# Attention and Fourier mixing on one core: where the row pass of the softmax throws its exponentials

## The chip, the cores and the metric

The kernel runs on 1 core of one Trainium2 chip. The metric is the device time of one execution in microseconds (us). Before the change it is 2742.67 us, the median of 3 runs (2741.53 to 2744.46).

## The reference, cut to what matters

```
# x: 2048 x 1024, 32 heads of 32, one key/value head for all of them
q = heads(x @ wq);  k = x @ wk;  v = x @ wv
scores = einsum("bhqd,bkd->bhqk", q, k) * 32 ** -0.5
p = softmax(scores, axis=-1)
a = heads_back(einsum("bhqk,bkd->bhqd", p, v)) @ wo
# a second, independent part on an input of its own (2048 x 1024)
y = seq_re @ (x2 @ hid_re) - seq_im @ (x2 @ hid_im)
out = concatenate([a, y], axis=-1)
```

Only the softmax is touched by the change. For each of the 32 x 2048 rows of scores it needs the row's largest score and the sum of the row's exponentials.

## The kernel before, in words

All work is written out in program order, engine by engine: the helper class `Ordered` (line 71) records every instruction, which is why the profile names one line, L79, for nearly all of them. Tiles are told apart by name instead.

The attention is cut into 32 *units* (4 blocks of 512 queries by 8 groups of 4 heads), and a unit into 32 *steps*, 1,024 in all. The main loop (line 941) runs one step n after the other, and does two things in a step, for two different units:

- **The row pass, ahead of time.** `score_step` (line 860) looks 44 steps ahead. `scores` (line 744) has TensorE make 128 queries x 1024 keys of scores in a PSUM tile `pss` (two matmuls; two such tiles exist), and VectorE takes each row's maximum into `nm`. One step later `row_sums` (line 755) has ScalarE take the exponential of that tile with the maximum as bias, with `accum_out` giving each row's sum. Only the sum is used. The exponentials themselves are thrown away: they are written back over the scores in `pss`. In the profile this instruction is a pair, ACTIVATE `pss<-pss,nm` and ACTIVATION_READ_ACCUMULATOR.
- **The exponentials by keys.** When a unit's row sums are known, `expo` (line 807) has TensorE make the scores again the other way round, 128 keys x 1024 queries, in the PSUM tile `pst` (two matmuls; only one such tile exists), and ScalarE takes their exponentials into an SBUF tile `p` (a pool `pp` of 13, line 719). In the profile: ACTIVATE `p<-pst`.

Within a step ScalarE's order is: the row pass of a step further ahead, then the exponentials by keys. TensorE's order is: the pss pair, the pst pair, then fill.

At steps 0, 12 and 22 of a unit, `pv` (line 821) has TensorE multiply the `p` tiles so far with the values: a *PV block* of 20 or 24 matmuls in the program, each of them two in the trace. This is what lets the `p` tiles go. Ahead of it, `aside` (line 405) may put up to six fill matmuls.

The *fill* is the rest of TensorE's work: projections, Fourier products and the output product, as matmuls `psb<-rh,mh` and the like. `level` (line 933) hands it out over the steps without a PV block, so that such a step holds four to six fill matmuls beside its pss and pst pairs. GpSimd prepares the fill's operands, SyncE's queue brings and takes data by DMA. The first 44 score steps run ahead of the main loop with seven fill matmuls each and without exponentials by keys; the last 44 steps of the main loop have no scores to make any more.

Order among instructions of different engines, and where a later instruction of the same engine overwrites what an earlier one wrote, is kept by semaphore waits that the tile layer puts in, one for each tile that is written or read.

Of the kernel before, what the change touches and what calls it, by code (L numbers as in the profile page):

```python
# [8 lines left out]
F32 = mybir.dt.float32  # L9
F32R = mybir.dt.float32r  # L10
AF = mybir.ActivationFunctionType
# [5 lines left out]
P = 128  # L17
# [4 lines left out]
W = 512  # L22
# [79 lines left out]
def tile_kernel(ctx: ExitStack, tc, xT, wq, wkv, wo, xbT, wT, cT, out):  # L102
    nc = tc.nc
    te = Ordered(tc, nc.tensor)
    act = Ordered(tc, nc.scalar)
# [5 lines left out]
    def pool(stack, name, bufs, **kw):  # L111
        kw.setdefault("reuse_waits", "tile")
        return stack.enter_context(tc.tile_pool(name=name, bufs=bufs, **kw))
# [36 lines left out]
    def move(q, to, of):  # L150
        q.dma_start(to.bitcast(F32), of.bitcast(F32))
# [125 lines left out]
    def add(gs):  # L277

        for g in gs:
            i0 = g.at = end[0]  # L280
            end[0] += g.n
            if groups and g.set[0] is not groups[-1].set[0]:
                prev["set"] = prev["this"]
                prev["this"] = i0
            for c, it in enumerate(g.right):
                if it.need is None:
                    it.need = i0 + 3 * c
                    p0 = min(prev["set"], i0 - it.back)
                    it.due = min(it.need, p0 + (i0 - p0) * (g.first + c + 1) // (len(g.set) * len(g.right))) - it.ahead
                    RL.items.append(it)  # L290
                it.last = i0 + 3 * c + 2
            for c, it in enumerate(g.left):
                if it.need is None:
                    it.need = it.due = i0 + 12 * c
                    ML.items.append(it)
                it.last = i0 + 12 * c + 11
            for it in g.ys:
                it.due = i0 + g.n
                ylist.append(it)
            groups.append(g)  # L300
# [31 lines left out]
    def store(to, of, key=None):  # L332
        def go():
            move(sp, to, of)
            if key:
                ready.add(key)
        soon(go)
# [240 lines left out]
    def wo_set(e):  # L578
        return [Item([(lambda g=g: wo[g * P:(g + 1) * P, e * W:(e + 1) * W], 1)]) for g in range(NG)]

    def o_left(b, t, q):
        g1 = min(q * 4 + 4, NQ * NG - 1 - b * NG)

        def src():
            assert all(("o", b, g) in ready for g in range(q * 4, g1)), (b, t, q)
            return [d[b][t][:, q * 4:g1] for d in (oh_d, ol_d)]
        return Item(None, pre=src)
# [82 lines left out]
    def o_group(b, t, e, ws):  # L670
        def post(ps):
            r0 = b * W + t * P
            to = out[r0:r0 + P, e * W:(e + 1) * W]
            if b < NQ - 1:
                oo = op.tile([P, W], F32, name="qh")
                dve.tensor_copy(oo, ps)
                store(to, oo)
                return

            n = len(halves)  # L680
            halves.append(n)
            oo = pp.tile([P, 2, W], F32, name="p")
            if n + 1 < 8:
                if n % 2:
                    dve.tensor_copy(oo[:, 0], ps)
                else:
                    act.activation(oo[:, 0], ps, AF.Copy)
                move(act, to, oo[:, 0])
                return
            for k, q in enumerate((act, sp)):  # L690
                cols = slice(k * W // 2, (k + 1) * W // 2)
                if k:
                    dve.tensor_copy(oo[:, k, :W // 2], ps[:, cols])
                else:
                    act.activation(oo[:, k, :W // 2], ps[:, cols], AF.Copy)
                move(q, to[:, cols], oo[:, k, :W // 2])
        return Group([o_left(b, t, q) for q in range(2)], ws, post)
# [21 lines left out]
    pp = pool(ctx, "pp", NP)  # L719
# [7 lines left out]
    qst, nm, lse, pt, ov, rb, pend = ({} for _ in range(7))  # L727
    ends = []

    def open_unit(u):  # L730
        b, g = units[u]
        assert ("q", b, g) in ready
        if u < 3:
            rows.append(qsp.tile([P, 4, W], F32R, name=f"qst{u}"))
            gp.memset(rows[u][96:P].bitcast(F32), 0.0)
        q = rows[u % 3]
        if u >= 3:
            move(sp, q[96:98].rearrange("p a b -> p (a b)"), kst[98:100])
        for r, src in enumerate((qh_d, ql_d, qh_d)):
            move(sp, q[r * DH:(r + 1) * DH], src[b][g].rearrange("(h d) c -> d h c", d=DH))  # L740
        qst[u] = q
        nm[u] = sm.tile([P, 10, NC], F32, name="nm")

    def scores(s):
        u, r = divmod(s, SU)
        i, j = divmod(r, 2)
        h, t = divmod(i, 4)
        ps = ps_s.tile([P, 2 * W], F32, name="pss")
        for a in range(2):
            k0 = (2 * j + a) * W  # L750
            te.matmul(ps[:, a * W:(a + 1) * W], qst[u][:, h, t * P:(t + 1) * P], kst[:, k0:k0 + W], start=True, stop=True)
        dve.tensor_reduce(nm[u][:, j, i:i + 1], ps, axis=AX.X, op=ALU.max, negate=True)
        pend[s] = ps

    def row_sums(s):
        if s not in pend:
            return
        ps = pend.pop(s)
        u, r = divmod(s, SU)
        i, j = divmod(r, 2)  # L760
        act.activation(ps, ps, AF.Exp, bias=nm[u][:, j, i:i + 1], accum_out=nm[u][:, 8 + j, i:i + 1])

    def over(rows):
        return rows.rearrange("p a c -> p c a")
# [21 lines left out]
    def lse_3(u):  # L786
        aside()
        pm = bank("psb")
        te.transpose(pm[:3 * NC, :P], nm[u][:, 3:6].rearrange("p a b -> p (a b)"), ident)
        mt = sm.tile([3 * NC, P], F32, name="mt")  # L790
        dve.tensor_copy(mt, pm[:3 * NC, :P])
        cur["at"] += 1
        lse[u] = mt
# [7 lines left out]
    def inverse(u):  # L801
        rb[u] = onp.tile([P, W], F32, name="rb")
        for h in range(4):
            r = r_d[u][4 * h:4 * h + 4].rearrange("t c -> (t c)")
            sp.dma_start(rb[u][h * DH:(h + 1) * DH], r.unsqueeze(0).to_broadcast([DH, W]))

    def expo(n):
        u, r = divmod(n, SU)
        c, hp_ = divmod(r, 2)
        pt[u, c, hp_] = pp.tile([P, 2, W], F32, name="p")  # L810
        ps = ps_t.tile([P, 2, W], F32, name="pst")
        for a in range(2):
            te.matmul(ps[:, a], kst[:, c * P:(c + 1) * P], qst[u][:, 2 * hp_ + a], start=True, stop=True)
        act.activation(pt[u, c, hp_], ps, AF.Exp)
# [45 lines left out]
    def score_step(s):  # L860

        if s < total:
            u, r = divmod(s, SU)
            if r == SU - 6 and u + 1 < len(units):
                open_unit(u + 1)
        if SU <= s < SU * (len(units) + 1) and s % SU == TURN:
            lse_3((s - SU) // SU)
        if s < total:
            scores(s)
        row_sums(s - 1)  # L870
        u, e = divmod(s - SU, SU)
        if 0 <= u < len(units):
            for f in LSE.get(e, ()):
                f(u)
# [58 lines left out]
    def level(n):  # L933
        r = n % SU
        if r in ENDS:
            return
        more = min(e for e in ENDS if e > r) - r
        left = goal(n + more) - pos["fill"]
        take(round(left / more))

    for n in range(total):
        u, r = divmod(n, SU)
        if n == total - 12:
            w1 = wo_set(1)
            add([o_group(NQ - 1, t, e, ws) for e, ws in ((0, w0), (1, w1)) for t in range(4)])
        score_step(n + SU + LEAD)
        if ends:
            ends.pop(0)()
        expo(n)
        if r == 16:  # L950
            inverse(u)
        if r in ENDS and n:
            pv((n - 1) // SU, (ENDS.index(r) - 1) % (len(CUT) - 1))
        level(n)
# [20 lines left out]
    def whole(i):  # L975
        if i % 5 < 2:
            return ps_s.tile([P, 2 * W], F32, name="pss")[:, :W]
        if i % 5 == 2:
            return ps_t.tile([P, 2, W], F32, name="pst")[:, 0]
        return ps_b[i % 5 - 3].tile([P, W], F32, name="psb")  # L980
# [9 lines left out]
    for t, g in enumerate(last[4:]):  # L990
        ps = whole(4 + t)
# [41 lines left out]
```

## Time and profile before

| | |
|---|---|
| median of 3 runs | 2742.67 us (2741.53 to 2744.46) |
| profiled execution, span from first to last instruction | 2740.7 us |
| mean granted TensorE clock in it | 1.000 |
| TensorE busy | 2733.4 us |
| ScalarE busy | 2159.8 us |
| GpSimd busy | 1721.8 us |
| VectorE busy | 1596.6 us |
| DMA queue q1, share of 16 engines | 61.6% |

The profile is of one execution of its own; its span is 2.0 us below the median of the timed runs. A matmul's busy time overlaps that of the next one, so that 100% says that TensorE always had a matmul begun, not that each ran at its best pace. In rows of the timeline the first number is the start in us from the span's start, the second the time until the last of the row's instructions ended; `[0.16 <-ACT p]` says that the engine stood idle 0.16 us ahead of it and that ScalarE's write of `p` ended that. In rows of groups, after the count stand the busy time in us and the mean of one in ns, then the idle time in front and what ended most of it. PEld is TensorE's weight load, which runs beside the matmul before it.

### The profile page before, as it was taken

The numbers are of one execution on the slowest core, as the hardware profiler recorded it, in microseconds if no ns is written. First come the engines' busy times: TensorE is split into PE (matmuls) and PEld (weight loads), VectorE is DVE, ScalarE is ACT, GpSimd is POOL, SyncE is SP. The second block draws the span as 40 slices with busy tenths as digits, with TensorE's granted clock in tenths as the row PEclk, the third lists the DMA queues.
The fourth block names the chain that finished last, engine by engine and source line by source line (L and its number), as shares of the span: only waits on it lengthen the run. The fifth ranks groups of instructions, "written<-read, shape, count | busy, mean of one in ns | idle before, by whom it ended". The sixth has DMA issues, their size and how long they took to land.

```text
span 2740.7 us, 40561 instructions
## 1 busy us (share of the span) xinstructions
PE 2733.4 (100%) x13820; PEld 1917.8 (70%) x13820; DVE 1596.6 (58%) x1826; ACT 2159.8 (79%) x3131; POOL 1721.8 (63%) x1711
## 2 busy tenths in 40 slices
PE   9999999999999999999999999999999999999999
PEld 6876767667676767667676776667676676767667
DVE  5766666666676666555565556666555555655411
ACT  3588878888887888888888888888888888888741
POOL 4854425777647558765556665576787887865751
PEclk9999999999999999999999999999999999999999
DMA  8643336887777666564354688874675765644565
GB/s 273 191 136 120 117 96 205 281 270 232 248 261 271 202 219 187 168 203 136 125 158 149 184 251 285 290 253 124 209 222 158 219 192 160 206 137 136 185 208 188
DMA packets 316931, 538.24 MB, mean 196 GB/s; under 512 B 35962, under 2 KB 63354, under 8 KB 316666
## 3 DMA queue, kind: packets, MB, share of 16 engines
q1 hardware_dynamic: 315572, 533.69, 61.6%
q8 instruction: 109, 1.79, 0.3%
q10 hardware_dynamic: 1152, 1.97, 0.2%
q14 instruction: 98, 0.80, 0.1%
HBM read 395.58 MB, written 138.15 MB: 195 GB/s over the span
## 4 chain that ended last, share of the span: by engine, by line
PE 98%; DMA 1%; SPq 0%; issue 0%; POOL 0%; ACT 0%; DVE 0%; DVEq 0%; POOLq 0%; ACTq 0%
PE psb L79 61%; PE pss L79 19%; PE pst L79 18%; DMA y<-u 0%; SPq L79 0%; DMA y<-c 0%; DMA qh<-in_wo_dram 0%; DMA rb<-r 0%; DMA m<-in_wq_dram 0%; POOL rl L79 0%; ACT p L79 0%; DVE y L79 0%; POOL ml L79 0%; DVE nm L79 0%; POOL m L79 0%
## 5 line engine op out<-in xcount | busy, mean ns | idle before, releaser
L79 DVE TENSOR_REDUCE nm<-pss 128x1 f32<-128x1024 f32 x1024 | 1252.8, 1224 | 572.5 <-PE pss L79 571.0
L79 ACT ACTIVATE p<-pst 128x1024 f32<-128x1024 f32 x1026 | 1056.0, 1029 | 449.7 <-PE pst L79 445.9
L79 ACT ACTIVATE pss<-pss,nm 128x1024 f32<-128x1024 f32 x1024 | 1116.0, 1090 | 61.3 <-DVE nm L79 59.2
L79 PE MATMUL psb<-rh,mh 128*128 128x512 f32 x1790 | 705.4, 394 | 1.0 <-DVE y L79 0.9
L79 PE MATMUL psb<-rh,ml 128*128 128x512 f32 x1790 | 704.2, 393 | 0.0
L79 PE MATMUL psb<-rl,mh 128*128 128x512 f32 x1790 | 704.0, 393 | 0.0
L79 PE MATMUL pss<-kst,qst 128*128 128x512 f32 x2048 | 653.7, 400 | 0.3
L79 PE MATMUL pst<-qst,kst 128*128 128x512 f32 x2048 | 650.3, 398 | 0.8 <-ACT p L79 0.7
L79 POOL TENSOR_TENSOR ml<-m,mh 128x512 fp32r<-128x512 f32 x366 | 471.8, 1289 | 35.8 <-ACT mh L79 26.5
L79 PEld LDWEIGHTS pss<-kst,qst 128*128 128x128 f32 x2048 | 374.6, 188 | 160.9 <-issue 76.3
L79 PE MATMUL psb<-p,v 128*32 128x512 f32 x4096 | 459.3, 594 | 0.0
L79 PEld LDWEIGHTS pst<-qst,kst 128*128 128x128 f32 x2048 | 374.9, 188 | 110.1 <-ACT p L79 26.1
L79 PEld LDWEIGHTS psb<-rh,mh 128*128 128x128 f32 x1790 | 336.2, 188 | 85.7 <-issue 2.4
L79 PEld LDWEIGHTS psb<-rl,mh 128*128 128x128 f32 x1790 | 336.1, 188 | 79.8 <-DVE rl L79 1.2
L79 PEld LDWEIGHTS psb<-rh,ml 128*128 128x128 f32 x1790 | 336.2, 188 | 79.0
L79 POOL CAST mh<-m 128x512 fp32r<-128x512 f32 x365 | 223.0, 611 | 245.9 <-PE psb L79 218.7
L79 PEld LDWEIGHTS psb<-p,v 128*32 128x32 f32 x4096 | 123.3, 110 | 283.7 <-issue 275.8
L79 POOL TENSOR_TENSOR m<-m,m 128x512 f32<-128x512 f32 x220 | 283.4, 1288 | 58.1 <-DMA m<-o 23.2
L79 POOL TENSOR_TENSOR rl<-r,rh 128x512 fp32r<-128x512 f32 x208 | 268.2, 1290 | 4.0
L79 POOL CAST rh<-r 128x512 fp32r<-128x512 f32 x208 | 127.5, 613 | 199.9 <-PE psb L79 149.6
L79 ACT ACTIVATION_READ_ACCUMULATOR pss<-pss,nm 128x1 f32 x1024 | 212.5, 207 | 0.0
L79 POOL TENSOR_TENSOR r<-r,r 128x512 f32<-128x512 f32 x120 | 154.8, 1290 | 72.8 <-DMA r<-in_wT_dram 44.8
(92 smaller groups left out, 790.5 us busy)
## 6 DMA issues: line engine op xcount, KB each, us to landing
m<-in_cT_dram SPq DMA_DIRECT2D x384, 256.0 KB
r<-s SPq DMA_DIRECT2D x192, 256.0 KB
y<-y SPq DMA_DIRECT2D x128, 256.0 KB
r<-in_wT_dram SPq DMA_DIRECT2D x88, 256.0 KB
m<-in_xbT_dram SPq DMA_DIRECT2D x88, 256.0 KB
y<-u SPq DMA_DIRECT2D x80, 256.0 KB
m<-in_wq_dram SPq DMA_DIRECT2D x64, 256.0 KB
qst<-qh SPq DMA_DIRECT2D x64, 256.0 KB
```

What stands on the lines that cost most here:

```text
L79: return lambda *a, **k: self.tc.keep_in_program_order(f(*a, **k))
```

## The change

`row_sums` no longer writes its exponentials back into `pss`, but into the SBUF tile `p` that the same step's `expo` fills with the exponentials by keys right afterwards. For that the main loop takes the `p` tile ahead of `score_step`, where before `expo` took it. Row passes ahead of the main loop (43 of 1,024) still write to `pss`. The same number of exponentials is taken of the same scores, and the sums come out of the same accumulator.

```
@@ row_sums
-        act.activation(ps, ps, AF.Exp, bias=nm[u][:, j, i:i + 1], accum_out=nm[u][:, 8 + j, i:i + 1])
+        to = spare.pop() if spare else ps
+        act.activation(to, ps, AF.Exp, bias=nm[u][:, j, i:i + 1], accum_out=nm[u][:, 8 + j, i:i + 1])
+
+    spare = []
@@ expo
-        pt[u, c, hp_] = pp.tile([P, 2, W], F32, name="p")
@@ the main loop
+        p = pt[u, r // 2, r % 2] = pp.tile([P, 2, W], F32, name="p")
+        spare[:] = [p.rearrange("p a b -> p (a b)")]
         score_step(n + SU + LEAD)
```

No instruction changes its place on any engine; what changes on ScalarE is a destination and the waits. This is ScalarE's order before, with the semaphores that each instruction waits for (PE, DVE, Activation for TensorE, VectorE and ScalarE itself), at the first steps of the second unit's row passes; `p_2244` and the like are numbered tiles:

```order
112 L79 ACTIVATE pss_2209,nm_2062<-pss_2209,nm_2062 128x1024 [waits DVE_49,Activation_49]
113 L79 ACTIVATE p_2244<-pst_2245 128x1024 [waits PE_49]
114 L79 ACTIVATE pss_2231,nm_2062<-pss_2231,nm_2062 128x1024 [waits DVE_49,Activation_49]
115 L79 ACTIVATE p_2278<-pst_2279 128x1024 [waits PE_49]
116 L79 ACTIVATE pss_2273,nm_2062<-pss_2273,nm_2062 128x1024 [waits DVE_49,Activation_49]
```

And the same place in the changed kernel:

```order
112 L79 ACTIVATE p_2231,nm_2063<-pss_2210,nm_2063 128x1024 [waits DVE_49]
113 L79 ACTIVATE p_2231<-pst_2245 128x1024 [waits PE_49,Activation_49]
114 L79 ACTIVATE p_2273,nm_2063<-pss_2232,nm_2063 128x1024 [waits DVE_49]
115 L79 ACTIVATE p_2273<-pst_2279 128x1024 [waits PE_49,Activation_49]
116 L79 ACTIVATE p_2300,nm_2063<-pss_2274,nm_2063 128x1024 [waits DVE_49]
```

Row pass and exponentials by keys of one step now write the same tile (`p_2231`, then `p_2273`). The wait for ScalarE's own semaphore has gone from the row pass, where it was for an earlier row pass that wrote the same one of two PSUM tiles, to the exponentials by keys, where it is for the row pass one row above.

This is ScalarE's order in the changed kernel a little later, around the step that follows the first PV block of that unit:

```order
156 L79 ACTIVATE p_2729,nm_2063<-pss_2703,nm_2063 128x1024 [waits DVE_49]
157 L79 ACTIVATE p_2729<-pst_2735 128x1024 [waits PE_49,Activation_49]
158 L79 ACTIVATE p_2766,nm_2063<-pss_2730,nm_2063 128x1024 [waits DVE_49,PE_49]
159 L79 ACTIVATE p_2766<-pst_2772 128x1024 [waits PE_49,Activation_49]
160 L79 ACTIVATE p_2783,nm_2063<-pss_2767,nm_2063 128x1024 [waits DVE_49]
```

The row pass in row 158 waits for TensorE as well, since its tile is the first one that this PV block lets go; there are 31 such rows in the kernel. Before, only the exponentials by keys that follow needed the tile.

## The prediction

> **What bounds the kernel now.** I read the page first: busy time, the chain, then the costliest groups.
>
> ```profile
> span 2740.7 us, 40561 instructions
> PE 2733.4 (100%) x13820; PEld 1917.8 (70%) x13820; DVE 1596.6 (58%) x1826; ACT 2159.8 (79%) x3131; POOL 1721.8 (63%) x1711
> PE 98%; DMA 1%; SPq 0%; issue 0%; POOL 0%; ACT 0%; DVE 0%; DVEq 0%; POOLq 0%; ACTq 0%
> L79 ACT ACTIVATE p<-pst 128x1024 f32<-128x1024 f32 x1026 | 1056.0, 1029 | 449.7 <-PE pst L79 445.9
> L79 ACT ACTIVATE pss<-pss,nm 128x1024 f32<-128x1024 f32 x1024 | 1116.0, 1090 | 61.3 <-DVE nm L79 59.2
> L79 PE MATMUL pst<-qst,kst 128*128 128x512 f32 x2048 | 650.3, 398 | 0.8 <-ACT p L79 0.7
> L79 ACT ACTIVATION_READ_ACCUMULATOR pss<-pss,nm 128x1 f32 x1024 | 212.5, 207 | 0.0
> ```
>
> TensorE is busy from end to end and is 98% of the chain; ScalarE is busy 79%. By that alone, nothing done to a ScalarE instruction could matter. But the share is an average over two kinds of step, so I looked next at the waits and the timeline. A step's row pass appears as two instructions, the exponential and the accumulator read; its exponentials by keys are the third.
>
> ```profile
> ACT p L79 <- PE pst L79: 445.9, 219, 5.4
> PEld pst L79 <- ACT p L79: 26.1, 114, 0.8
> 1499.25 1.03 ACT L79 ACTIVATE p<-pst 128x1024 f32<-128x1024 f32 x1 [3.44 <-PE pst L79]
> ```
>
> ScalarE's idle time lies almost all in 219 long waits, up to 5.4 us, like the 3.44 us ahead of 1499.25: the steps in which TensorE runs a block of weighted sums (PV). There are 3 of these in 32 steps. And the weight load for pst already waits for ScalarE 114 times. An ordinary step looks like this (timeline, ScalarE and TensorE rows only):
>
> ```profile
> 1508.52 1.08 ACT L79 ACTIVATE pss<-pss,nm 128x1024 f32<-128x1024 f32 x1
> 1509.03 0.63 PE L79 MATMUL pst<-qst,kst 128*128 128x512 f32 x2
> 1509.52 0.20 ACT L79 ACTIVATION_READ_ACCUMULATOR pss<-pss,nm 128x1 f32 x1
> 1509.70 1.03 ACT L79 ACTIVATE p<-pst 128x1024 f32<-128x1024 f32 x1
> 1510.62 1.08 ACT L79 ACTIVATE pss<-pss,nm 128x1024 f32<-128x1024 f32 x1
> 1510.88 0.42 PEld L79 LDWEIGHTS pst<-qst,kst 128*128 128x128 f32 x2
> 1511.12 0.63 PE L79 MATMUL pst<-qst,kst 128*128 128x512 f32 x2
> ```
>
> From one pst pair to the next is 2.09 us: nine matmuls of 0.23 us (two pss, two pst, five of the fill). ScalarE has nothing free in it: its row pass begins 0.11 us before the exponentials end (1510.62 against 1510.73). So in ordinary steps the two engines run almost even; who is slower is decided by less than 0.1 us. The fastest that ScalarE can go today shows where it is behind:
>
> ```profile
> 363.61 0.31 PEld L79 LDWEIGHTS pst<-qst,kst 128*128 128x128 f32 x2 [0.16 <-ACT p L79]
> 363.72 0.63 PE L79 MATMUL pst<-qst,kst 128*128 128x512 f32 x2
> 365.44 1.10 ACT L79 ACTIVATE pss<-pss,nm 128x1024 f32<-128x1024 f32 x1
> 365.81 0.62 PE L79 MATMUL pst<-qst,kst 128*128 128x512 f32 x2
> 366.43 0.22 ACT L79 ACTIVATION_READ_ACCUMULATOR pss<-pss,nm 128x1 f32 x1
> 366.53 1.04 ACT L79 ACTIVATE p<-pst 128x1024 f32<-128x1024 f32 x1
> 367.43 1.11 ACT L79 ACTIVATE pss<-pss,nm 128x1024 f32<-128x1024 f32 x1
> 367.62 0.30 PEld L79 LDWEIGHTS pst<-qst,kst 128*128 128x128 f32 x2 [0.24 <-ACT p L79]
> 367.66 0.69 PE L79 MATMUL pst<-qst,kst 128*128 128x512 f32 x2
> ```
>
> A cycle takes 2.01 us (load released at 363.61 and, two cycles on, at 367.62). Here TensorE alternates steps of 2.09 and 1.85 us (363.72, 365.81, 367.66), and where the load had stood idle 0.24 us the pst pair took 0.69 instead of 0.63 us: that is TensorE losing time to ScalarE, a little, already. A load that stood idle 0.16 us cost nothing.
>
> **The change part by part.** The row pass's arithmetic, operands read, and place in every queue stay; no matmul, DMA, VectorE or GpSimd instruction is added or moved. Three things change.
>
> *1. A wait inside ScalarE, on the path.* Both exponentials of a step now write one tile, so the second must wait until the first is complete (the order shows it: the exponentials by keys gain a wait on ScalarE's own semaphore; the row pass loses one on a row pass two steps older, long done, worth nothing). When is the first complete? Another reader shows it:
>
> ```profile
> 1811.28 0.19 ACT L79 ACTIVATION_READ_ACCUMULATOR pss<-pss,nm 128x1 f32 x1
> 1811.37 1.01 ACT L79 ACTIVATE p<-pst 128x1024 f32<-128x1024 f32 x1
> 1811.53 0.30 PEld L79 LDWEIGHTS pss<-kst,qst 128*128 128x128 f32 x2 [0.58 <-ACT pss L79]
> ```
>
> TensorE, waiting for the row pass, is let go only behind the accumulator read (end 1811.47, load 1811.53), while ScalarE's next exponentials began at 1811.37, 0.10 us before that end, as at 366.53 against 366.65. That overlap goes, and a release is added. The release: at 1509.66 the pst pair ends and at 1509.70 the exponentials start, 0.04 us. So a ScalarE cycle becomes: start of row pass to end of its accumulator read 1.20 (1508.52 to 1509.72), release 0.04, start of exponentials to start of the next row pass 0.92 (1509.70 to 1510.62): 2.16 us instead of 2.01. What is queued behind the wait on ScalarE is the next row pass; what waits for it is the load for pst (one buffer, so TensorE can't start the next pst pair).
>
> *2. A wait taken one step part earlier.* The tile is taken before the row pass, so that now waits for the PV block to release it: in the order 31 row passes wait for TensorE, each right behind the first PV block of a unit. In that step ScalarE waits for TensorE anyway (3.44 us in the row above), so I price it at nothing. Without that cover it would be at most some 1.5 us (six fill matmuls of 0.23 ahead of the PV block) on 31 steps, 47 us; the cover is twice as long.
>
> *3. The destination itself.* No row of this trace has the row pass writing to SBUF. Bound from the rows: the exponentials by keys, same shape, PSUM to SBUF, take 1029 ns against 1090; that would make the row part 0.06 us shorter, if the difference is the destination's and not the accumulator's or the bias operand's. The other way:
>
> ```profile
> L79 ACT ACTIVATE rh<-p 128x512 fp32r<-128x512 f32 x10 | 6.2, 627 | 1.1 <-DMA p<-in_xT_dram 1.0
> L79 ACT ACTIVATE p<-psb 128x512 f32<-128x512 f32 x1 | 0.6, 598 | 5.1 <-PE psb L79 5.1
> ```
>
> With SBUF in place of PSUM as source, 627 against 598: 0.03 us longer; the same for a destination is an estimate. I take 0: what counts is when the accumulator read ends, and its own 0.2 us are started by the arithmetic's end (1509.52, 0.08 before the row pass's own end), which the destination doesn't touch. Ends for the range: cycle 2.10 and 2.19. The Trainium skill speaks against the change here: "ScalarE: Activation LUTs", under the step-by-step section, calls PSUM the faster destination for ScalarE. It gives no time; by the 0.03 above the sum would be 2.19.
>
> A release through a separate waiting instruction is slower than 0.04, and the exponentials now have two waits, so one is separate. The row pass has that form today:
>
> ```profile
> 99.82 1.23 DVE L79 TENSOR_REDUCE nm<-pss 128x1 f32<-128x1024 f32 x1 [0.86 <-PE pss L79]
> 101.14 1.09 ACT L79 ACTIVATE pss<-pss,nm 128x1024 f32<-128x1024 f32 x1 [0.88 <-DVE nm L79]
> ```
>
> 0.09 us from the maximum's end (101.05) to 101.14, against 0.04. I take it that the separate one is TensorE's: then a step in which ScalarE waits for TensorE starts its exponentials 0.05 later, and the cycle stays 2.16. If it is ScalarE's, the cycle is 2.21.
>
> *What the cycle does to TensorE.* The pst pairs give the steps' lengths; these are the first and the last of 1,024 (2,048 matmuls in the page's row):
>
> ```profile
> 137.56 0.62 PE L79 MATMUL pst<-qst,kst 128*128 128x512 f32 x2
> 2680.89 0.67 PE L79 MATMUL pst<-qst,kst 128*128 128x512 f32 x2
> ```
>
> Read off the timeline, 95 of the 1,023 intervals hold a PV block (5 to 7.6 us), 40 at the end hold no row pass, and 888 in 92 unbroken stretches are ordinary: 700 of nine matmuls (2.09 us), 60 of eight (1.86), 109 of ten (2.31), 19 longer. With a cycle of 2.16, a nine-matmul step puts ScalarE 0.07 behind, an eight-matmul step 0.30; a ten-matmul step gives back 0.15, a PV block everything. Each stretch can absorb some lag: at 1510.73 the exponentials end and the load for pst would come at 1510.88; less the 0.06 that a load takes after its release (1811.47 to 1811.53) that is 0.09; some 0.13 more that I chose, since a load idle for 0.16 cost nothing and one idle for 0.24 cost 0.07; less the 0.05 above: 0.17. Roughly: 700 x 0.07 + 60 x 0.30 = 67 us of lag, 92 x 0.17 = 16 absorbed, leaves 51 if no long step ever meets a lag, 35 if each ten-matmul step does (109 x 0.15 = 16). Walking the 92 stretches in order (lag plus cycle minus step, never below 0; what exceeds 0.17 is TensorE's loss) gives 44.1 us at 2.16. The same walk at today's 2.01 gives 1.1, so 43.0 is new. At other cycles: 2.10 gives 10.8, 2.12 gives 19.1, 2.18 57.4, 2.19 64.1, 2.21 79.4.
>
> **The sum.** 2740.7 + 43 = 2783.7 for the profiled execution. The median of the runs, 2742.67, lies 2.0 above its span: 2786 us, 1.6% slower. A measurement of this kernel can tell about 0.2% (5.5 us) from no change.
>
> **The rivals.**
>
> *The wait is free (0.10; 2743 us, no change).* This is the other side: the exponentials would start behind the row pass as they do now. For it: TensorE is 98% of the chain, and the wait is on the engine's own instruction just ahead. Against it: 366.53 is 0.12 before the accumulator read's end at 366.65, so an overlap exists to be lost, and the load at 1811.53 shows that completion is told at that end. It decides from a cycle of about 2.07, where less than 5.5 us is left; that needs a release of less than nothing. The Trainium skill has a rule that would give this result if it held for ScalarE: "VectorE: DVE Perf Modes", on the drain that can't be avoided, found eight copies equally long with a semaphore after each and with one at the end. It is stated of VectorE; the rows of ScalarE above overlap, so I follow them.
>
> *The SBUF destination ends the row part sooner (0.19; 2752 us).* Cycle 2.10: 10.8 - 1.1 = 9.7 more. For it: 1029 against 1090 ns. Against it: the accumulator read is a second instruction whose start follows the arithmetic. Its own range is 2.07 to 2.13, 2748 to 2767.
>
> *The row part gets longer, or the release is the slow form (0.17; 2806 us).* Cycle 2.19: 64.1 - 1.1 = 63. For it: 627 against 598, 0.09 against 0.04. Its range is 2.18 to 2.22, 2799 to 2830. The skill's rule on destinations, above, is on this side.
>
> *Faster (0.02; 2735 us).* The cycle would have to fall below 2.01, the row part by more than 0.15 us, when the nearest row allows 0.06; and then only what the kernel loses to ScalarE now is to be had: 1.1 by the walk, some 8 if the late loads in steps without row passes count as well.
>
> **How the numbers follow.** The forecast (cycle 2.13 to 2.18, 2767 to 2799, likeliest 2786) has 0.52. The range 2746 to 2815 leaves out the no-change case, the faster one and the top of the slow one, some 0.2 together. Slower by over 0.2%: 0.52 + 0.19 + 0.17, less 0.02 for the bottom of the short case, 0.86; within 0.2%: 0.12; faster: 0.02.
>
> **What the new profile would show.** Right: the exponentials by keys start at or some 0.03 us behind the accumulator read's end, never before; in stretches of ordinary steps the row passes start 2.15 us apart and TensorE's steps with them; the wait of pst's weight load for ScalarE grows from 114 times and 26 us to some 500 times and over 100; ScalarE's idle time moves from ahead of PV steps to between row pass and exponentials; PV steps are as long as now. Wrong: the exponentials still start ahead of the accumulator read's end (then step 1 falls); the row part is 1.14 or 1.23 instead of 1.20 (then step 3); row passes wait for TensorE in the first ordinary step after a PV block and the load for pss waits there (then step 2).

## The result, and the profile after

The changed kernel takes 2776.75 us, the median of 4 runs (2775.51 to 2777.26), against 2742.10 us before (4 runs, 2741.41 to 2744.46): a ratio of 1.0123, 95% interval 1.0108 to 1.0137. That is 1.2% or 34.7 us slower, where 43 us were forecast. The profiled execution has a span of 2775.3 us against 2740.7, 34.6 us more.

These are lines of the changed kernel's page, and below them two lines of its waits; they answer to the lines of the same groups shown of before.

```profile
span 2775.3 us, 40589 instructions
PE 2764.2 (100%) x13820; PEld 1889.7 (68%) x13820; DVE 1598.0 (58%) x1826; ACT 2197.7 (79%) x3131; POOL 1725.5 (62%) x1711
PE 97%; DMA 1%; ACT 1%; DVE 1%; issue 0%; SPq 0%; DVEq 0%; ACTq 0%
L79 ACT ACTIVATE p<-pst 128x1024 f32<-128x1024 f32 x1026 | 1053.4, 1027 | 445.5 <-PE pst L79 415.8
L79 ACT ACTIVATE p<-pss,nm 128x1024 f32<-128x1024 f32 x981 | 1088.2, 1109 | 12.0 <-PE psb L79 7.1
L79 PE MATMUL pst<-qst,kst 128*128 128x512 f32 x2048 | 670.0, 408 | 2.6 <-ACT p L79 1.3
```

```profile
ACT p L79 <- PE pst L79: 415.8, 155, 5.2
PEld pst L79 <- ACT p L79: 114.1, 441, 0.9
```

The shares tell nothing: TensorE 100% busy and nearly the whole chain, ScalarE 79%, as before. Two smaller figures tell it. The weight load for pst waits for ScalarE 441 times and 114.1 us (114 times and 26.1 us before), and a pst matmul takes 408 ns on the mean instead of 398: its 2,048 matmuls hold 670.0 - 650.3 = 20 us more of "busy" time, in pairs like the one at 370.57 below, which begins together with its late weight load and takes 0.73 us where 0.63 is usual. The rest shows as later starts. The timeline of the changed kernel, in a stretch of ordinary steps, ScalarE's rows and the pst rows of TensorE:

```profile
369.49 1.03 ACT L79 ACTIVATE p<-pst 128x1024 f32<-128x1024 f32 x1
370.42 1.11 ACT L79 ACTIVATE p<-pss,nm 128x1024 f32<-128x1024 f32 x1
370.57 0.30 PEld L79 LDWEIGHTS pst<-qst,kst 128*128 128x128 f32 x2 [0.45 <-ACT p L79]
370.57 0.73 PE L79 MATMUL pst<-qst,kst 128*128 128x512 f32 x2
371.41 0.20 ACT L79 ACTIVATION_READ_ACCUMULATOR p<-pss,nm 128x1 f32 x1
371.64 1.03 ACT L79 ACTIVATE p<-pst 128x1024 f32<-128x1024 f32 x1
372.57 1.11 ACT L79 ACTIVATE p<-pss,nm 128x1024 f32<-128x1024 f32 x1
372.72 0.30 PEld L79 LDWEIGHTS pst<-qst,kst 128*128 128x128 f32 x2 [0.23 <-ACT p L79]
374.88 0.30 PEld L79 LDWEIGHTS pst<-qst,kst 128*128 128x128 f32 x2 [0.46 <-ACT p L79]
```

The exponentials start 0.03 us behind the accumulator read's end (371.61, 371.64); before, they started 0.12 ahead of it (366.53 against 366.65). The row passes start 2.15 us apart (370.42, 372.57), and the weight loads for pst are let go 2.15 us apart (370.57, 372.72, 374.88). TensorE's steps follow ScalarE's pace here, not its own.

Where the exponentials do wait for TensorE, behind a PV block, the release is the slower one:

```profile
383.84 0.63 PE L79 MATMUL pst<-qst,kst 128*128 128x512 f32 x2
384.57 1.03 ACT L79 ACTIVATE p<-pst 128x1024 f32<-128x1024 f32 x1 [4.34 <-PE pst L79]
```

The pair ends at 384.47 and they start 0.10 us later; before, it was 0.04 (1509.66, 1509.70).

Where in a unit the time went can be worked out from the pst pairs of the two timelines: the interval from each pair to the next, after less before, added up over the 32 units by the step's number. In the steps 1 to 4, 13 to 16 and 23 to 25, those right behind a PV block, the sum is 0.2 us in all. The other 21 of the 32 steps hold the remaining 34.4 us. So a PV block wipes the lag out, the first three or four steps absorb what builds up anew, and most of the steps after them cost.

### The profile page after: what moved, and what is told of

It is laid out like the page before. It is cut to its first block, busy times and chain, and to the rows that moved or that the text cites. A ratio compares the mean times of both kernels' runs of the same rounds, so it can differ in the third digit from the quotient of the medians.

```text
span 2775.3 us, 40589 instructions
## 1 busy us (share of the span) xinstructions
PE 2764.2 (100%) x13820; PEld 1889.7 (68%) x13820; DVE 1598.0 (58%) x1826; ACT 2197.7 (79%) x3131; POOL 1725.5 (62%) x1711
## 4 chain that ended last, share of the span: by engine, by line
PE 97%; DMA 1%; ACT 1%; DVE 1%; issue 0%; SPq 0%; DVEq 0%; ACTq 0%
PE psb L79 60%; PE pss L79 19%; PE pst L79 19%; ACT p L79 1%; DMA out_dram<-y 0%; DVE nm L79 0%; DMA y<-u 0%; DMA y<-c 0%; DVE y L79 0%; SPq L79 0%; DMA m<-in_wq_dram 0%; ACT pss L79 0%; DVE rl L79 0%; ACT rh L79 0%; DVE qh L79 0%
## 5 line engine op out<-in xcount | busy, mean ns | idle before, releaser
L79 ACT ACTIVATE p<-pst 128x1024 f32<-128x1024 f32 x1026 | 1053.4, 1027 | 445.5 <-PE pst L79 415.8
L79 ACT ACTIVATE p<-pss,nm 128x1024 f32<-128x1024 f32 x981 | 1088.2, 1109 | 12.0 <-PE psb L79 7.1
L79 PE MATMUL pst<-qst,kst 128*128 128x512 f32 x2048 | 670.0, 408 | 2.6 <-ACT p L79 1.3
L79 PEld LDWEIGHTS pst<-qst,kst 128*128 128x128 f32 x2048 | 347.4, 188 | 171.2 <-ACT p L79 114.1
L79 ACT ACTIVATION_READ_ACCUMULATOR p<-pss,nm 128x1 f32 x981 | 196.5, 200 | 0.0
```

What stands on the lines that cost most here:

```text
L79: return lambda *a, **k: self.tc.keep_in_program_order(f(*a, **k))
```

## The experiments

Three theories were open. *The wait*: ScalarE's own wait between its two exponentials makes its cycle 2.15 us instead of 2.01, and TensorE pays what this exceeds a stretch's slack. *The destination*: writing to SBUF is what costs. *The early tile*: the row pass behind a unit's first PV block has to wait for that block. Each run has its own runs of before beside it, on the same chip, and the ratio is to those.

**The destination without the wait.** The row pass writes to the tile that the *next* step's exponentials will fill.

```
+        for m in range(n, n + 1 + (r != 12 and n + 1 < total)):
+            um, rm = divmod(m, SU)
+            if (um, rm // 2, rm % 2) not in pt:
+                pt[um, rm // 2, rm % 2] = pp.tile([P, 2, W], F32, name="p")
+        p = pt[um, rm // 2, rm % 2]
+        spare[:] = [p.rearrange("p a b -> p (a b)")] if m > n else []
```

> The row pass still writes to SBUF, but into the tile that the next step's exponentials by keys will fill, so that the wait on ScalarE's own semaphore is for a row pass one whole step back (in the step whose next tile isn't free yet, one in 32, it writes to PSUM). Theory of the wait: the exponentials start again ahead of the accumulator read's end, the cycle is about 2.01 us, and the time is that of before, 2742 us, or up to 4 more for the second wait's separate instruction. Theory of the destination (writing 1024 exponentials to SBUF costs ScalarE's cycle the time): the destination is unchanged, so the time stays at that of the changed kernel, 2777 us.

Measured: 2744.56 us (10 runs), ratio 1.0006 (0.9997 to 1.0016). Its timeline, ScalarE's rows:

```profile
363.76 1.11 ACT L79 ACTIVATE p<-pss,nm 128x1024 f32<-128x1024 f32 x1
364.76 0.20 ACT L79 ACTIVATION_READ_ACCUMULATOR p<-pss,nm 128x1 f32 x1
364.85 1.03 ACT L79 ACTIVATE p<-pst 128x1024 f32<-128x1024 f32 x1
365.75 1.12 ACT L79 ACTIVATE p<-pss,nm 128x1024 f32<-128x1024 f32 x1
```

Its groups by line, the row passes into `p`:

```profile
L79 ACT ACTIVATE p<-pss,nm 128x1024 f32<-128x1024 f32 x950 | 1058.9, 1115 | 15.2 <-PE psb L79 9.3 <-DVE nm L79 4.4
```

950 row passes write to SBUF, each a little longer than those to PSUM, and the time is that of before, within 2 us. The exponentials start 0.11 us ahead of the accumulator read's end again (364.85 against 364.96), and the row passes 1.99 us apart. The early tile is in this kernel too (row passes wait 9.3 us for psb, 7.1 in the changed kernel), and so are the two waits of the exponentials; what differs is that ScalarE's own wait is for a row pass one step back. The destination is out.

**The wait without the destination, by a bias.** The exponentials by keys take as bias the sum that the row pass just ahead has made; in the control the sum of the row pass before that, `sums[-2]`.

```
+        sums.append(nm[u][:, 8 + j, i:i + 1])
...
-        act.activation(pt[u, c, hp_], ps, AF.Exp)
+        act.activation(pt[u, c, hp_], ps, AF.Exp, bias=sums[-1])
```

> The kernel before, row pass into PSUM as ever, but the exponentials by keys take as bias the row sum that the row pass just ahead of them made (so they come out changed; the rest of the work is the same). This puts the wait in without the destination. Theory of the wait: cycle 2.15 us, time that of the changed kernel, 2777 us, within 6. Theory of the destination: 2742 us.

> The control for the wait alone: the bias is the sum of the row pass one step earlier, so that the operand is there and the wait is for something long done (the exponentials by keys come out changed in the same manner). Theory of the wait: 2742 us, up to 4 more. If the bias operand itself lengthens the exponentials, this run shows by how much, and the difference between the two runs is the wait.

Measured: 2845.54 us with the wait (ratio 1.0374, 1.0359 to 1.0390) and 2761.39 in the control (1.0066, 1.0051 to 1.0081). Both lie outside what was expected, by 63 and by 15 us. The groups of the one with the wait, the exponentials by keys:

```profile
L79 ACT ACTIVATE p<-pst,nm 128x1024 f32<-128x1024 f32 x1024 | 1144.2, 1117 | 429.9 <-PE pst L79 402.2 <-PE psb L79 0.2
```

Its timeline, ScalarE's rows:

```profile
431.00 1.08 ACT L79 ACTIVATE pss<-pss,nm 128x1024 f32<-128x1024 f32 x1
432.00 0.20 ACT L79 ACTIVATION_READ_ACCUMULATOR pss<-pss,nm 128x1 f32 x1
432.23 1.12 ACT L79 ACTIVATE p<-pst,nm 128x1024 f32<-128x1024 f32 x1
433.25 1.08 ACT L79 ACTIVATE pss<-pss,nm 128x1024 f32<-128x1024 f32 x1
```

The timeline of the control, two weight loads in a row for pst:

```profile
366.00 0.30 PEld L79 LDWEIGHTS pst<-qst,kst 128*128 128x128 f32 x2 [0.36 <-ACT p L79]
368.10 0.30 PEld L79 LDWEIGHTS pst<-qst,kst 128*128 128x128 f32 x2 [0.18 <-ACT p L79]
```

A bias that is an operand in SBUF makes the exponentials 1117 ns instead of 1027, so the pair had two costs in it, not one. The cycles are 2.24 us over a stretch of nine (431.00 to 433.25 is 2.25) with the wait and 2.10 (366.00 to 368.10) without, 0.14 apart, as between the changed kernel and before. The difference of the two, 84 us, is the wait's price from a cycle of 2.10 upward, where little slack is left; it is not its price in the kernel. The next experiment puts the wait in without a longer instruction.

**The wait without the destination, by one column.** The exponentials go to PSUM as before; only the one column of row sums goes to the tile `p`. The kernel's own columns for the sums are filled with 1.

```
+        gp.memset(nm[u][:, 8:], 1.0)
...
-        to = spare.pop() if spare else ps
-        act.activation(to, ps, AF.Exp, bias=nm[u][:, j, i:i + 1], accum_out=nm[u][:, 8 + j, i:i + 1])
+        to = spare.pop()[:, :1] if spare else nm[u][:, 8 + j, i:i + 1]
+        act.activation(ps, ps, AF.Exp, bias=nm[u][:, j, i:i + 1], accum_out=to)
```

> The wait alone, without a longer instruction: the row pass writes its 1024 exponentials to PSUM as before; only its row sums, one column, go to the tile that the same step's exponentials by keys overwrite (so the row sums are left out, their columns are set to 1 once in a unit). Theory of the wait: the exponentials start 0.03 us behind the accumulator read's end, cycle 2.15 us, time that of the changed kernel, 2777 us, within 4. Theory of the destination: 2743 us.

Measured: 2776.80 us, ratio 1.0125 (1.0110 to 1.0141): the changed kernel's time to 0.1 us. Its groups, the row passes (input and product in PSUM):

```profile
L79 ACT ACTIVATE pss<-pss,nm 128x1024 f32<-128x1024 f32 x1024 | 1109.8, 1084 | 59.8 <-DVE nm L79 39.3 <-POOL ml L79 12.5 <-PE psb L79 7.1
```

A line of its waits (us in all, times, us of the longest), and its timeline:

```profile
PEld pst L79 <- ACT p L79: 114.0, 442, 0.8
```

```profile
368.38 1.08 ACT L79 ACTIVATE pss<-pss,nm 128x1024 f32<-128x1024 f32 x1
369.37 0.20 ACT L79 ACTIVATION_READ_ACCUMULATOR pss<-pss,nm 128x1 f32 x1
369.61 1.03 ACT L79 ACTIVATE p<-pst 128x1024 f32<-128x1024 f32 x1
370.53 1.08 ACT L79 ACTIVATE pss<-pss,nm 128x1024 f32<-128x1024 f32 x1
```

Row passes are 1084 ns, those of PSUM; the exponentials start behind the accumulator read (369.57, 369.61); cycle 2.15; the load for pst waits 442 times and 114.0 us, against 441 and 114.1. One shared column makes the whole effect. The early tile is in this kernel as well, with the same 7.1 us for psb as in the changed one; the next experiment takes it out of the changed kernel. (The 12.5 us for ml are a single wait, at the start.)

**The early tile.** The 31 row passes that wait for a PV block write to PSUM.

```
-        spare[:] = [p.rearrange("p a b -> p (a b)")]
+        spare[:] = [p.rearrange("p a b -> p (a b)")] if r != 13 else []
```

> The changed kernel, but the row passes of the step behind each unit's first PV block, the 31 that wait for TensorE to release their tile, write to PSUM as before. Theory of the wait: these 31 steps have no wait on the row pass just ahead, so 1 to 2 us less than the changed kernel, 2775 us. Theory of the early tile (ScalarE is held up by the release and TensorE then by ScalarE, once in each unit): most of the 35 us come back, 2745 to 2755 us.

Measured: 2773.40 us, ratio 1.0111 (1.0094 to 1.0128), beside 1.0123 (1.0108 to 1.0137) for the changed kernel. The intervals overlap; at most a few us come back, not most of the 35. Two of the few are seen in its timeline, by the same sums as above: the steps 17 and 18, where a stretch's lag passes its slack, cost 1.3 us instead of 3.1, for each of these stretches begins with one wait less. The theory of the early tile falls.

**A price for each wait, or a threshold.** Every second step's row pass goes back to PSUM.

```
-        spare[:] = [p.rearrange("p a b -> p (a b)")]
+        spare[:] = [p.rearrange("p a b -> p (a b)")] if n % 2 else []
```

> The changed kernel with every second step's row pass back in PSUM. Theory of a threshold (only what ScalarE's lag exceeds the slack of a stretch is lost): cycles of 2.15 and 2.01 us take turns, 2.08 on the mean, just under the 2.09 us of TensorE's common step, so lag hardly builds up: 6 to 9 us above before, 2748 to 2751 us. Theory of a price for each wait (each of the 981 waits costs its 0.035 us): half of the 35 us, 2759 us.

Measured: 2749.49 us (10 runs), ratio 1.0024 (1.0014 to 1.0033): 6.6 us above before, for half of the waits. A price for each would make it 17. Two cycles of this kernel, one without the wait and one with it:

```profile
366.51 1.08 ACT L79 ACTIVATE pss<-pss,nm 128x1024 f32<-128x1024 f32 x1
367.60 1.03 ACT L79 ACTIVATE p<-pst 128x1024 f32<-128x1024 f32 x1
368.50 1.13 ACT L79 ACTIVATE p<-pss,nm 128x1024 f32<-128x1024 f32 x1
369.75 1.03 ACT L79 ACTIVATE p<-pst 128x1024 f32<-128x1024 f32 x1
370.67 1.08 ACT L79 ACTIVATE pss<-pss,nm 128x1024 f32<-128x1024 f32 x1
```

1.99 and 2.17 us, 2.08 on the mean, below TensorE's 2.09.

**The other side of the threshold.** Before, with a row pass that has no bias operand.

```
-        act.activation(ps, ps, AF.Exp, bias=nm[u][:, j, i:i + 1], accum_out=nm[u][:, 8 + j, i:i + 1])
+        act.activation(ps, ps, AF.Exp, scale=0.001, accum_out=nm[u][:, 8 + j, i:i + 1])
```

> The kernel before with the row pass made shorter: no bias operand (the exponentials that are summed are of a thousandth of the score, unshifted, so the sums come out changed). The earlier pair of runs had an exponential with such an operand 0.09 us longer than one without. If so, the row pass takes about 1.00 us instead of 1.09 and a cycle 1.92. Theory of a threshold (TensorE sets the end, ScalarE costs only what it lags): just what before loses to ScalarE comes back, 1 to 4 us, 2739 to 2742 us. Theory of a price for each instruction of ScalarE: 981 times 0.09 us, 2655 us.

Measured: 2739.29 us (11 runs), ratio 0.9988 (0.9980 to 0.9997): 3.1 us (0.1%) faster. Its row passes take 1020 ns (1090 before), by its groups:

```profile
L79 ACT ACTIVATE pss<-pss 128x1024 f32<-128x1024 f32 x1024 | 1044.7, 1020 | 65.4 <-DVE nm L79 63.3
```

A line of its waits:

```profile
PEld pst L79 <- ACT p L79: 20.2, 100, 0.8
```

The page's busy time for the group fell by 1116.0 - 1044.7 = 71 us, and the kernel by 3.

**What before already loses.** In the last 43 steps the exponentials by keys get their PSUM tile from the pool of two.

```
+        if n > total - SU - LEAD:
+            ps = ps_s.tile([P, 2 * W], F32, name="pss").rearrange("p (a b) -> p a b", a=2)
+        else:
+            ps = ps_t.tile([P, 2, W], F32, name="pst")
```

> The kernel before, with one thing against the waits for ScalarE that it already has: in the last 43 steps, which make no scores for a row pass, the exponentials by keys take their PSUM tile from the pool of two that the scores left free, in place of the one pst tile. If the late weight loads there cost what their lateness beyond some 0.13 us sums to, this is 1 to 3 us below before, 2739 to 2741 us: hardly to be told from no change. If they cost nothing, 2742 us.

Measured: 2740.17 us (11 runs), ratio 0.9992 (0.9983 to 1.0001): 2.8 us below before, which the interval can't quite tell from nothing.

**All together.** ScalarE's shortest cycle against what the kernel takes over its own runs of before, and what the walk of the prediction gives for that cycle (less the 1.1 us that it gives for 2.01):

| kernel | cycle, us | measured, us | walk, us |
|---|---|---|---|
| no bias operand | about 1.92 (the shortest distance of two row passes) | -3.1 | -1.1 |
| before | 2.01 | 0 | 0 |
| next step's tile | 2.01 | +1.8 | 0 |
| every second step | 2.08 on the mean | +6.6 | 5.9 |
| bias, no wait | 2.10 | +18.7 | 9.7 |
| changed kernel | 2.15 | +34.7 | 36 |
| column only | 2.15 | +34.4 | 36 |
| bias and wait | 2.24 | +102.8 | 104 |

The cycle is the distance at which the weight loads are let go while ScalarE runs without a pause. The curve is nearly flat up to TensorE's common step of 2.09 us and then rises, by 0.4 us for each ns from 2.08 to 2.15 (28.1 us over 70 ns) and by 0.76 from 2.15 to 2.24 (68.1 over 90), whatever makes the cycle long. One point lies off the walk, the bias without the wait: there the exponentials end 0.09 us later in their own step as well, which uses up half of the slack; with 0.08 instead of 0.17 the walk gives 13.4, and the 5 us that are still missing are left open. The half slack itself is argued and not shown: the kernel with bias and wait has the same later end, and there 0.08 gives 111 where 102.8 were measured.

## Why the prediction was right, point by point

- **What bounds the kernel.** Right: two engines within 0.1 us of each other in the 700 nine-matmul steps of the 888 ordinary ones, under shares of 100% and 79%. Shown by the curve: 71 us less of ScalarE's work gave back 3, and 0.14 us more in a cycle cost 35. One row was misread on the way: the 219 waits for the pst pairs are not all in PV steps. Sorted by the pst pairs, the 95 steps with a PV block hold 385 of the 446 us, the steps at the end without a row pass 36, and the rest is short waits in ordinary steps. The sum doesn't use the 219.
- **Step 1, the wait.** Right, and shown by itself: the column-only kernel has the wait without the destination, and the changed kernel's time; the next step's tile has the destination without the wait, and the time of before. The three parts of the cycle came out as read from before: row part 1.20 (370.42 to 371.61 is 1.19), release 0.03 where 0.04 was taken, exponentials to the next row pass 0.93 (371.64 to 372.57). The slow release fell to TensorE's wait, as assumed (0.10 at 384.57 against 0.04, where 0.05 more was taken), and not to ScalarE's own.
- **Step 2, the early tile.** Right in the main: priced at nothing. The waits exist (12 row passes wait for psb, 7.1 us in all), the sign that was named against this step shows a little (the load for pss waits for p 3 times, 2.5 us in all), and the run without them came out 3.3 us lower, with overlapping intervals; 1.8 us of it can be seen in the steps' lengths. Since the kernel that takes its tiles yet a step earlier, but without ScalarE's own wait, costs 1.8 us over before (0.9997 to 1.0016), the early tile alone costs no more than some 4.
- **Step 3, the destination.** Right that it doesn't count, and for the reason given: to SBUF the row pass is 1109 ns, to PSUM 1084 (column only), but the accumulator read ends 1.19 to 1.20 us after the row pass's start in both (370.42 to 371.61; 368.38 to 369.57), so nothing behind it moves. The lower end of the range, that 1029 against 1090 was the destination's, was wrong: that difference is the bias operand's. The Trainium skill's rule in "ScalarE: Activation LUTs" (step-by-step section) that PSUM is the faster destination agrees with the 25 ns. The Trainium skill gives the operand's price in the same page, "ScalarE: Activation LUTs", under what ACT_TABLE_LOAD costs: some 0.093 us for each operand of one value a partition. The rows here give 0.090 (1117 against 1027), which agrees, and 0.070 the other way (1090 against 1020), which is less.
- **The sum.** Too high by 8 us, in two terms. The cycle was added up from rounded rows as 2.16 and is 2.15 (release 0.03): the walk at 2.152 gives 37.7. The slack, 0.17, was partly chosen; with 0.20 the walk at 2.152 gives 35.7, which is 1 us above the 34.7 measured. That 0.17 was too small for this kernel is fitted, not shown by a run of its own; the bias kernel without the wait points the other way.
- **The rivals.** The free wait falls with the column-only kernel, and with it the thought that the Trainium skill's rule in "VectorE: DVE Perf Modes", on the drain that can't be avoided, might hold for ScalarE: here the semaphore is what takes the overlap away (0.12 us ahead of the accumulator read's end without it, 0.03 behind with it). The shorter and the longer row part both fall with the 1.19 to 1.20. Faster was not to be had: 3 us is what a shorter cycle gives.
- **What the profile was to show.** Weight loads waiting "some 500 times and over 100 us": 441 and 114.1. ScalarE's waits for the pst pairs: 445.9 to 415.8 us, 219 to 155 times; its idle time ahead of the exponentials that is not put down to them rose from 3.8 (449.7 - 445.9) to 29.7 us (445.5 - 415.8), so some 26 us moved to between row pass and exponentials, and the greater part stayed where it was. PV steps were to stay as they were; by the pst pairs they are 2.5 us longer in all (the 91 ahead of the last 44 steps, 6.23 to 6.26 us on the mean), lag that reaches into them.

## What to carry to other kernels

ScalarE's neighbouring instructions overlap at their ends here, by 0.12 us, and sharing a destination between two of them, if only one column, ended that overlap: throw results away into something that the engine's next instruction doesn't touch. Whether this costs is not read from shares of busy time: compare the engine's shortest cycle with the bound engine's step, stretch by stretch, since here 0.09 us less below that step gave back 3 us, while 0.09 more above it cost 68. An experiment that puts in a wait by adding an operand has to be paired with one that adds the operand alone, and even then the difference is right only at its own distance from the threshold.

## What the runs showed of the hardware that wasn't expected

- A bias that is an operand makes a 128x1024 exponential 0.09 us longer (1117 against 1027 ns), and ScalarE's cycle as much (2.01 to 2.10), which the prediction had not taken into account; taking it away from the row pass made that 0.07 shorter (1090 to 1020).
- ScalarE writing 128x1024 to SBUF instead of PSUM ends 25 ns later (1109 against 1084 ns, both with the wait in the kernel), without delaying the accumulator read behind it.
- While ScalarE runs back to back, its instructions' recorded times grow along a stretch though their starts keep their distance (before: 1.10 us at 365.44, 1.11 at 367.43, 1.99 apart), and what waits for an end moves with it (the weight loads at 363.61 and 367.62, 2.01 a cycle). Where the exponentials wait for the row pass ahead, row passes keep one length: 1.11 us to SBUF, 1.08 to PSUM (column only). A mean over a back-to-back group (1115 ns in the kernel with the next step's tile) is then too high for what the instruction alone takes.
